# Both layernorms' normalised rows written with backward column chunks, and a new order of the units

## The chip, the core and the metric

The kernel runs on one core of one Trainium2 chip. The metric is the device time in microseconds (us), the median of several executions. Before the change it is 290.33 us (three runs, 290.32 to 290.42). One profiled execution took 287.78 us; inside it the hardware profiler's span, from the first recorded instruction to the last, is 286.0 us. Times of single instructions below come from that profile.

## The reference

One transformer block over 2048 tokens of 640 columns, in bf16. Cut to what matters:

```python
x = A_x                                          # [1, 2048, 640]
h = x + A(layernorm(x), wqkv, w_phi, wo)         # linear attention, 32 heads of 20
h2 = h + B(layernorm(h), w_gate, w_up, w_down)   # gated MLP, 1536 wide, no nonlinearity

# A: q, k, v = split(x @ wqkv); phi(q) = [softmax(q w_phi), softmax(-q w_phi)], phi(k) alike
#    kv = sum_s phi_k^T v;  z = sum_s phi_k;  o = (phi_q kv) / (phi_q z + 1e-6);  return o @ wo
# B: return ((x @ w_gate) * (x @ w_up)) @ w_down
```

The layernorm has no weights: (x - mean) / sqrt(var + 1e-5).

## The kernel before

The 2048 tokens are 16 tiles of 128 rows (NT); the 640 columns are 5 chunks of 128 (NC). Everything stays in on-chip memory between input and output.

The work of one tile t in the first part, with the names that the kernel gives to its units:

- L1s, L1a (VectorE, L398 to L401): mean and variance; L1l, L1e (ScalarE, L406, L409): 1/sqrt as exp(-0.5 ln v).
- xn (VectorE, L426): (x - mean) * rs, written as one row of 640 bf16 into one of four buffers.
- xt: transposes the row's five 128 x 128 blocks into xnT, chunk by chunk, so that the columns lie on the partitions. Tiles 0 to 2 on TensorE (L434, moved out of PSUM by xte), tiles 3 to 15 by a DMA transpose on SyncE's queue (L442).
- V and K (TensorE, L455): xnT's chunk c as the stationary operand, weight chunk c as the moving one, accumulated over c. For tiles 0 and 1 they are split into five units each (V0_0 to V0_4 and so on), so that each can start when its weight chunk is ready. K's and Q's weights are first multiplied by w_phi on the chip: WT transposes K's weights (L361), WTe moves them out of PSUM, F1 and F0 are the products (L382), Fe moves the result out.
- Ve moves V to SBUF; Kx makes both exponentials (ScalarE, L476); Ks and Kr are sum and reciprocal (VectorE, L479, L482); Kn divides (GpSimd, L484); KV adds the tile's phi_k^T v into three PSUM banks that live through all 16 tiles (TensorE, L493).

The second part: Q (L514) with its exponentials Qx; per tile N, the two numerator products (L547), a chain of small VectorE units (sr, rho, A, B, dd, rd), the division o (L579), a DMA transpose oT (L584), O times wo (L590), the residual h (L594), statistics L2s, L2a, and hc (ScalarE, L609): mean - h, written into the same four row buffers as xn. hT (L614) transposes it by DMA into xnT. The MLP runs over blocks of 256, 512, 512, 512 and 256 tokens: U (L629) gives gate and up products, g copies one (L634), u multiplies both (L637), D is the down product (L648), y scales by the row's -1/std and adds the residual (L660), w stores (L662).

The order is planned when the program is built. Each unit is entered with an engine, a cost (occupancy and latency in us), what it reads and writes, and a key. A table of text, TUNED, gives the key of each of 975 units, and with ":1" that the second of its possible engines is used. schedule (L687) is a list scheduler: it walks through modelled time, and whenever an engine is free it takes the ready unit with the lowest key. The keys are planned start times, so the engines' queues follow them. emit then puts semaphore waits between the queues; each engine works through its queue strictly in order, so a unit that waits holds up all behind it. The modelled costs never reach the chip; only the order and the choice of engine do. The function that gives the cost of a plain copy is the pattern for the others:

```python
def dve_c(n, psum=False):
    return 0.065 + n / 960.0 + (0.02 if psum else 0.0)
```

The functions that the change touches follow.

Of the kernel before, what the change touches and what calls it, by code (L numbers as in the profile page):

```python
# [12 lines left out]
P = 128  # L13
# [35 lines left out]
x0:0.7 wk0:4.06 wk2:3.58 wk4:2.14 x1:2.62 wv0:4.54 wv2:5.5 wv4:1.18 x2:5.02 x4:5.98 x6:6.46 phr:1.66 ph50:1 ph5:3.1 x8:15.6 x10:20.94 x12:26.78  # L49
x14:25.08 wqt0:25.56 wqt1:22.64 wqt2:31.25 wqt3:34.65 wqt4:38.91 wqt5:37.69 wo0:42.61 wo2:43.09 wg0:33.69 wu0:34.17 wg1:50.56 wu1:48.38 wg2:47.9  # L50
wu2:50.08 wg3:51.52 wu3:51.04 wg4:53.22 wu4:53.7 id0:0.7 gl0:1.2 eps:1.45 id1:2.97 gla0:3.97 glb0:4.41 gla4:1.87 glb4:2.31 gla1:1.65 glb1:4.19
gla2:2.09 glb2:2.75 gla3:2.53 glb3:4.63 phi0:4.85 phi5:6.053 va1:3.37 glx:6.304 kv1:6.704 zero:0.7 warm:1.08 WT0:7.553 WTe0:8.195 WT1:7.218
WTe1:8.902:1 WT2:6.883 WTe2:7.488 WT3:6.246 WTe3:6.851 WT4:4.63 WTe4:5.235 F1_0:9.36 Fe1_0:10.21:1 F1_1:9.933 Fe1_1:10.81 F1_2:10.507 Fe1_2:11.41:1
F1_3:7.916 Fe1_3:8.908:1 F1_4:6.581 Fe1_4:8.156 L1s0:3.163 L1a0:4.193 L1s1:5.583 L1a1:6.613 L1s2:10.51 L1a2:12.36 L1s3:9.66 L1a3:12.21 L1s4:14.2
L1a4:16.05 L1s5:11.36 L1a5:15.05 L1s6:12.51 L1a6:16.2 L1s7:15.2 L1a7:16.35 L1s8:19.58 L1a8:20.98 L1s9:21.13 L1a9:23.38 L1s10:24.93 L1a10:27.73
L1s11:25.78 L1a11:27.88 L1s12:32.77 L1a12:36.44 L1s13:38.54 L1a13:41.21 L1s14:41.36 L1a14:42.76 L1s15:35.02 L1a15:36.29 L1l0:4.523 L1e0:4.883
L1l1:6.943 L1e1:7.303 L1l2:12.69 L1e2:13.05 L1l4:16.68 L1e4:17.04 L1l8:28.21 L1e8:28.96 L1l12:43.091 L1e12:44.502 xn0:5.163 xt0:5.763 xte0:6.312
xn1:7.736 xt1:8.336 xte1:9.609 xn2:13.36 xt2:14.069 xte2:14.667 xn3:13.78 xt3:14.38 xn4:18.74 xt4:19.72 xn5:17.9 xt5:18.5 xn6:18.32 xt6:23.86 xn7:19.16
xt7:21.42 xn8:29.43 xt8:30.03 xn9:35.87 xt9:36.47 xn10:40.79 xt10:41.39 xn11:31.8 xt11:32.47 xn12:44.86 xt12:45.46 xn13:45.28 xt13:46.68 xn14:47.65
xt14:48.86 xn15:49.47 xt15:52 V0_0:9.088 V0_1:9.662 V0_2:10.235 V0_3:10.809 V0_4:11.352 Ve0:12.011 K0_0:11.08 K0_1:11.895 K0_2:12.439 K0_3:12.982  # L60
K0_4:13.525 Kx0_0:14.067 Kx0_1:15.268 Ks0:16.5 Kr0:20.43 Kn0:21.16 KV0:30.691 V1_0:12.71 V1_1:13.254 V1_2:13.797 V1_3:14.348 V1_4:14.891 Ve1:15.868
K1_0:11.624 K1_1:12.167 K1_2:14.619 K1_3:15.163 K1_4:20.911 Kx1_0:21.834 Kx1_1:22.644 Ks1:23.53 Kr1:27.18 Kn1:29.719 KV1:32.725 V2:16.836 Ve2:18.52
K2:15.478 Kx2_0:17.11 Kx2_1:17.92 Ks2:21.98 Kr2:26.63 Kn2:27.36 KV2:34.76 V3:19.553 Ve3:21.233 K3:18.194 Kx3_0:19.823 Kx3_1:20.633 Ks3:30.4 Kr3:32.22
Kn3:34.437 KV3:38.152 V4:26.616 Ve4:28.36 K4:23.899 Kx4_0:25.58 Kx4_1:26.39 Ks4:33.62 Kr4:37.99 Kn4:38.72 KV4:41.545 V5:21.183 Ve5:23.244 K5:22.541
Kx5_0:24.169 Kx5_1:24.98 Ks5:28.03 Kr5:29.85 Kn5:32.078 KV5:43.579 V6:27.974 Ve6:29.603 K6:31.367 Kx6_0:33.671 Kx6_1:34.482 Ks6:36.59 Kr6:42.21
Kn6:42.94 KV6:46.972 V7:25.258 Ve7:26.991 K7:29.333 Kx7_0:31.637 Kx7_1:32.447 Ks7:39.39 Kr7:44.31 Kn7:45.299 KV7:47.95 V8:33.401 Ve8:35.082 K8:35.436
Kx8_0:37.064 Kx8_1:37.874 Ks8:42.91 Kr8:47.1 Kn8:47.83 KV8:51.747 V9:42.221 Ve9:43.902 K9:40.187 Kx9_0:42.491 Kx9_1:43.301 Ks9:45.7 Kr9:50.44
Kn9:52.979 KV9:56.498 V10:45.614 Ve10:47.294 K10:44.255 Kx10_0:45.884 Kx10_1:46.694 Ks10:48.07 Kr10:49.89 Kn10:50.62 KV10:57.476 V11:36.794 Ve11:38.475
K11:38.828 Kx11_0:40.457 Kx11_1:41.267 Ks11:50.99 Kr11:52.57 Kn11:55.338 KV11:58.453 V12:52.423 Ve12:54.051 K12:49.03 Kx12_0:50.658 Kx12_1:51.469
Ks12:53.129 Kr12:54.709 Kn12:57.697 KV12:61.846 V13:55.139 Ve13:56.82 K13:50.388 Kx13_0:52.069 Kx13_1:52.879 Ks13:55.488 Kr13:57.068 Kn13:60.056  # L70
KV13:62.824 V14:60.488 Ve14:62.168 K14:53.781 Kx14_0:55.409 Kx14_1:56.22 Ks14:57.847 Kr14:59.427 Kn14:62.415 KV14:67.017 V15:63.5 Ve15:65.128:1
K15:59.129 Kx15_0:60.758 Kx15_1:61.568 Ks15:62.378 Kr15:63.958 Kn15:64.774 KV15:68.772 KVe0:69.718 KVe1:70.328 KVe2:70.938 F0_0:58.152 Fe0_0:58.723
F0_1:57.174 Fe0_1:57.746 F0_2:62.522 Fe0_2:63.094 F0_3:48.626 Fe0_3:49.198 F0_4:47.648 Fe0_4:48.22 Q0_0:70.527 Qx0_0_0:72.37 Qx0_0_1:71.876 Q0_1:65.937
Qx0_1_0:67.287 Qx0_1_1:67.78 Q0_2:69.448 Qx0_2_0:71.291 Qx0_2_1:70.797 Q0_3:67.693 Qx0_3_0:69.535 Qx0_3_1:69.042 Q0_4:64.858 Qx0_4_0:66.207
Qx0_4_1:66.701 Q1_0:78.727 Qx1_0_0:80.076 Qx1_0_1:80.57 Q1_1:87.595 Qx1_1_0:89.51 Qx1_1_1:89.016 Q1_2:82.309 Qx1_2_0:84.152 Qx1_2_1:83.659 Q1_3:86.516
Qx1_3_0:90.004 Qx1_3_1:88.523 Q1_4:75.879 Qx1_4_0:77.721 Qx1_4_1:77.228 Q2_0:77.648 Qx2_0_0:79.491 Qx2_0_1:78.997 Q2_1:92.881 Qx2_1_0:94.23
Qx2_1_1:94.724 Q2_2:73.03 Qx2_2_0:74.379 Qx2_2_1:74.873 Q2_3:91.112 Qx2_3_0:93.638 Qx2_3_1:92.461 Q2_4:90.033 Qx2_4_0:91.876 Qx2_4_1:91.382 Q3_0:79.806
Qx3_0_0:81.155 Qx3_0_1:81.649 Q3_1:84.747 Qx3_1_0:86.59 Qx3_1_1:86.096 Q3_2:74.799 Qx3_2_0:76.642 Qx3_2_1:76.149 Q3_3:71.606 Qx3_3_0:73.449
Qx3_3_1:72.955 Q3_4:80.885 Qx3_4_0:82.234 Qx3_4_1:82.728 wd0:96.508 wd1:95.068 wd2:96.028 wd3:95.548 N0_1:72.685 N0_0:74.109 sr0:73.3 rho0:74.724
A0:75.023 B0:75.988 dd0:76.953 rd0:77.251 o0:77.731 oT0:79.152 O0:83.389 h0:85.118 L2s0:86.049 L2a0:87.509 L2v0:88.96 L2r0:89.708 hc0:87.839 hT0:88.733  # L80
N1_1:77.303 N1_0:76.958 sr1:77.918 rho1:78.408 A1:78.706 B1:79.671 dd1:80.636 rd1:80.934 o1:81.414:1 oT1:82.326 O1:88.674 h1:90.486 L2s1:91.418
L2a1:92.448 L2v1:92.778 L2r1:93.128 hc1:92.955 hT1:93.848 N2_1:86.171 N2_0:85.826 sr2:86.899 rho2:87.659 A2:87.958 B2:88.923 dd2:89.888 rd2:90.186
o2:90.666 oT2:92.087 O2:95.664 h2:97.544 L2s2:98.476 L2a2:99.506 L2v2:99.836 L2r2:100.186 hc2:99.836 hT2:100.777 N3_1:81.964 N3_0:74.454 sr3:82.579
rho3:83.069 A3:83.368 B3:84.333 dd3:85.869 rd3:87.209 o3:87.689 oT3:89.953 O3:93.96 h3:95.643 L2s3:96.694 L2a3:98.296 L2v3:98.626 L2r3:99.326
hc3:98.664 hT3:99.557 N4_1:92.191 N4_0:92.536 sr4:92.806 rho4:93.296 A4:93.594 B4:94.559 dd4:95.524 rd4:96.394 o4:96.874 oT4:98.295 O4:106.256
h4:107.884 L2s4:109.368 L2a4:110.569 L2v4:110.899 L2r4:111.853 hc4:111.03 hT4:111.923 N5_1:99.205 N5_0:95.319 sr5:99.82 rho5:100.31 A5:100.609
B5:101.809 dd5:102.946 rd5:103.478 o5:103.958 oT5:105.379 O5:109.252 h5:111.101 L2s5:112.324 L2a5:113.525 L2v5:113.855 L2r5:114.455 hc5:114.034
hT5:114.927 N6_1:103.716 N6_0:103.371 sr6:104.331 rho6:104.821 A6:105.291 B6:106.256 dd6:107.221 rd6:107.519 o6:108.636:1 oT6:109.548 O6:114.575
h6:116.799 L2s6:117.73 L2a6:118.88 L2v6:120.331 L2r6:120.681 hc6:119.21 hT6:120.104 N7_1:133.568 N7_0:115.934 sr7:134.183 rho7:134.673 A7:134.971
B7:135.936 dd7:136.901 rd7:137.199 o7:137.679:1 oT7:138.591 O7:143.236 h7:144.908 L2s7:145.969 L2a7:146.999 L2v7:147.329 L2r7:147.934 hc7:147.329  # L90
hT7:148.223 N8_1:138.229 N8_0:140.733 sr8:139.118 rho8:141.643 A8:141.941 B8:142.906 dd8:144.309 rd8:144.608 o8:145.088 oT8:146.509 O8:151.782
h8:153.41 L2s8:154.342 L2a8:155.372 L2v8:155.702 L2r8:156.052 hc8:155.702 hT8:156.595 N9_1:144.939 N9_0:144.594 sr9:145.659 rho9:146.819 A9:147.149
B9:148.623 dd9:150.026 rd9:150.824 o9:151.304 oT9:152.725 O9:156.4 h9:158.029 L2s9:159.09 L2a9:160.12 L2v9:160.45 L2r9:161.055 hc9:160.45 hT9:161.344
N10_1:112.248 N10_0:112.593 sr10:113.675 rho10:114.337 A10:114.877 B10:116.014 dd10:117.55 rd10:118.58 o10:119.06 oT10:121.324 O10:161.709 h10:163.37
L2s10:164.854 L2a10:165.884 L2v10:166.214 L2r10:166.564 hc10:166.214 hT10:167.107 N11_1:176.039 N11_0:178.543 sr11:176.654 rho11:179.158 A11:179.456
# [106 lines left out]
def act_c(n, ptr=False):  # L202
    return (0.15 if ptr else 0.067) + n / 1200.0


def pool_c(n):
    return 0.183 + 0.0017 * n
# [801 lines left out]
```

## Time and profile before

| | |
|---|---|
| median time | 290.33 us |
| span of the profile | 286.0 us |
| TensorE busy, matmuls | 277.0 us, 2083 |
| VectorE busy | 184.4 us |
| ScalarE busy | 108.8 us |
| GpSimd busy | 58.9 us |
| xn (L426), 16 instructions | 13.0 us busy, mean 842 ns |
| hc (L609), 16 instructions | 13.1 us busy, mean 824 ns |
| Kn (L484), 16 instructions | 37.5 us busy, mean 2368 ns |

How to read the profile: it has a page (busy times, the span in slices, the chain of work that ended last, groups of instructions by line) and answers to questions about the trace. A line of the waits reads "engine, tile, line <- who ended the wait: us in total, times, longest". A line of the timeline reads "start, length, engine, line, operation, output <- input, shapes, count", with the idle time before it in brackets. PE is TensorE, PEld its weight loads, DVE VectorE, ACT ScalarE, POOL GpSimd, SPq SyncE's queue of transfers. Recorded matmuls overlap, so a busy TensorE may still be short of its best rate.

### The profile page before, as it was taken

The page shows a single profiled execution, that of the slowest core. Times are in us where ns is not written, and L with a number is a line of the kernel's source. Part 1 is how long each engine was busy: PE and PEld are TensorE (multiplying, and loading weights), DVE is VectorE, ACT ScalarE, POOL GpSimd, SP SyncE. Part 2 cuts the span into 40 slices and gives each one's busy share as a digit, 9 for nine tenths or more (in the row PEclk, how much of TensorE's full clock was granted, in tenths as well). Part 3 has the DMA queues.
Part 4 walks back from the last instruction along what each step waited for, and adds up shares of the span by engine and source line. Part 5 has one row for each costly group of instructions (what it writes and reads, how often), then busy time and mean ns, then how long its engine had stood idle before and what let it go on. Part 6 is the DMA issues. An engine that isn't in the chain of part 4 may idle for free.

```text
span 286.0 us, 5034 instructions
## 1 busy us (share of the span) xinstructions
PE 277.0 (97%) x2083; PEld 182.0 (64%) x2083; DVE 184.4 (64%) x364; ACT 108.8 (38%) x191; POOL 58.9 (21%) x66
## 2 busy tenths in 40 slices
PE   6899998999999999999999999998999999999996
PEld 2677776877555588854456774564456544678875
DVE  5799999985378888942588781587342373652342
ACT  4778555754877842321321112212340022022310
POOL 7003847699110321020003000001000000100000
PEclk9999999999999999999999999999999999999999
DMA  6737587990021397330013323015200110122002
GB/s 172 246 88 152 131 206 135 245 303 37 0 20 28 71 293 98 59 78 6 0 23 49 92 58 60 0 23 72 46 1 28 44 23 2 46 37 80 2 0 69
DMA packets 44832, 22.31 MB, mean 78 GB/s; under 512 B 35977, under 2 KB 43529, under 8 KB 44809
## 3 DMA queue, kind: packets, MB, share of 16 engines
q1 hardware_dynamic: 44809, 21.99, 33.5%
q8 instruction: 16, 0.26, 0.4%
q14 instruction: 7, 0.06, 0.1%
HBM read 11.00 MB, written 2.62 MB: 48 GB/s over the span
## 4 chain that ended last, share of the span: by engine, by line
PE 82%; DVE 6%; POOL 5%; DMA 4%; ACT 1%; issue 0%; SPq 0%; DVEq 0%; POOLq 0%
PE ps L629 36%; PE ps L648 18%; PE ps L514 8%; PE ps L455 7%; PE ps L590 7%; POOL ev L484 4%; PE ps L547 4%; DVE xn L426 3%; DVE SR L479 2%; DMA scratch<-scratch 2%; DMA scratch<-in_A_wqkv_dram 2%; DMA xnT<-xn 1%; PE ps L493 1%; DVE SR L482 1%; PE ps L382 1%; PE ps L361 1%
## 5 line engine op out<-in xcount | busy, mean ns | idle before, releaser
L629 PE MATMUL ps<-xnT,Wgu 128*128 128x512 bf16 (+1 forms) x600 | 107.8, 336 | 0.0
L629 PEld LDWEIGHTS ps<-xnT,Wgu 128*128 128x128 bf16 x600 | 58.3, 98 | 41.9 <-DVE ev L637 0.4
L634 ACT ACTIVATE scratch<-ps 128x512 bf16<-128x512 f32 (+1 forms) x60 | 30.7, 512 | 94.5 <-PE ps L629 84.7
L637 DVE TENSOR_TENSOR ev<-ps,scratch 128x512 bf16<-128x512 f32 (+1 forms) x60 | 33.4, 576 | 34.2 <-ACT scratch L634 23.5
L648 PE MATMUL ps<-Wp,ev 128*128 128x320 bf16 (+2 forms) x396 | 54.0, 295 | 0.0
L455 PE MATMUL ps<-Wp,xnT 128*128 128x320 bf16 x320 | 46.2, 299 | 1.5 <-DMA xnT<-xn 1.5
L648 PEld LDWEIGHTS ps<-Wp,ev 128*128 128x128 bf16 x396 | 38.0, 98 | 14.6
L484 POOL TENSOR_TENSOR ev<-ev,SR 128x1280 bf16<-128x1280 bf16 x16 | 37.5, 2368 | 27.9 <-DVE mv L401 16.7
L455 PEld LDWEIGHTS ps<-Wp,xnT 128*128 128x128 bf16 x320 | 30.2, 98 | 13.7 <-DMA xnT<-xn 2.4
L579 POOL TENSOR_TENSOR scratch<-scratch,sm 128x640 bf16<-128x640 f32 x10 | 12.7, 1273 | 123.7 <-DVE sm L576 110.2
L660 DVE SCALAR_TENSOR_TENSOR Wp<-ps,rs,x_all 128x640 bf16<-128x640 f32 (+3 forms) x18 | 14.6, 810 | 26.2 <-PE ps L648 26.1
L609 ACT ACTIVATE xn<-x_all,mv 128x640 bf16<-128x640 bf16 x16 | 13.1, 824 | 37.8 <-DVE mv L603 37.5
L476 ACT ACTIVATE ev<-ps 128x640 bf16<-128x640 f32 x32 | 21.0, 701 | 13.3 <-PE ps L455 9.2
L590 PE MATMUL ps<-Wo,scratch 128*128 128x320 bf16 x160 | 24.0, 299 | 1.3 <-DMA scratch<-scratch 1.3
L479 DVE TENSOR_REDUCE SR<-ev 128x64 f32<-128x1280 bf16 x16 | 23.4, 1461 | 2.8 <-ACT ev L476 2.1
L523 ACT ACTIVATE eqT<-ps 128x512 bf16<-128x512 f32 x40 | 21.7, 594 | 8.5 <-PE ps L514 8.5
L514 PE MATMUL ps<-xnT,Wp 128*128 128x512 bf16 x100 | 23.4, 379 | 0.0
L590 PEld LDWEIGHTS ps<-Wo,scratch 128*128 128x128 bf16 x160 | 15.5, 98 | 8.3 <-DMA scratch<-scratch 1.7
L560 DVE RECIPROCAL sm<-ps 128x32 f32<-128x32 f32 x16 | 5.6, 352 | 16.0 <-PE ps L547 15.9
L594 DVE TENSOR_TENSOR x_all<-ps,x_all 128x640 bf16<-128x640 f32 x16 | 13.1, 821 | 4.2 <-PE ps L590 4.1
L514 PEld LDWEIGHTS ps<-xnT,Wp 128*128 128x128 bf16 x100 | 9.5, 97 | 9.4
L547 PEld LDWEIGHTS ps<-KVm,eqT 128*128 128x128 bf16 x192 | 12.8, 98 | 4.1
(55 smaller groups left out, 204.6 us busy)
## 6 DMA issues: line engine op xcount, KB each, us to landing
out_dram<-Wp SPq DMA_DIRECT2D x15, 160.0 KB, 1.8
x_all<-in_A_x_dram SPq DMA_DIRECT2D x7, 320.0 KB, 4.2
Wgu<-in_B_w_gate_dram SPq DMA_DIRECT2D x5, 384.0 KB, 5.7
Wgu<-in_B_w_up_dram SPq DMA_DIRECT2D x5, 384.0 KB, 4.1
Wp<-in_B_w_down_dram SPq DMA_DIRECT2D x4, 480.0 KB, 5.7
scratch<-in_A_wqkv_dram SPq DMA_DIRECT2D x2, 320.0 KB, 4.8
Wp<-in_A_wqkv_dram SPq DMA_DIRECT2D x2, 320.0 KB, 5.8
Wo<-in_A_wo_dram SPq DMA_DIRECT2D x1, 480.0 KB, 4.3
```

The lines of the kernel that those rows point to most:

```text
L455: ins = e.matmul(pb(b, hb)[:, 0:320], lhsT=T["xnT"][:, c, P * t:P * (t + 1)], rhs=T["Wp"][:, kind, c, 320 * hb:320 * (hb + 1)], start=(c = ...
L476: G.op("act", "Kx%d_%d" % (t, s), lambda e, s=s, b=b, ek=ek: e.activation(out=T["ek"][:, ek.slots[0], s, :].rearrange("p (b n) -> p b n", ...
L479: G.op("dve", "Ks%d" % t, lambda e, ek=ek, sr=sr: e.tensor_reduce(out=T["SR"][:, sr.slots[0], 0, :], in_=T["ek"][:, ek.slots[0], :, :].rea ...
L484: G.op("pool", "Kn%d" % t, lambda e, ek=ek, sr=sr: e.tensor_tensor(out=T["ek"][:, ek.slots[0], :, :].rearrange("p s (h f) -> p (s h) f", f ...
L514: ins = e.matmul(pb(b)[:, 0:n], lhsT=T["Wp"][:, 0, i, P * c:P * (c + 1)], rhs=T["xnT"][:, i, o0:o0 + n], start=(i == 0), stop=(i == NC - 1))
L523: G.op("act", "Qx%d_%d_%d" % (q, c, s), lambda e, s=s, c=c, o0=o0, n=n, b=b: e.activation(out=T["eqT"][:, s, c, o0:o0 + n], in_=pb(b)[:, 0 ...
L547: ins = e.matmul(pb(b, y)[:, 22 * h0:22 * (h0 + j1 - j0)], lhsT=T["eqT"][:, s, c, P * t:P * (t + 1)], rhs=T["KVm"][:, OFF[s, c] + j0:OFF[s ...
L590: ins = e.matmul(pb(b, hb)[:, 0:320], lhsT=T["oT"][:, oT.slots[0], c, :], rhs=T["Wo"][:, c, 320 * hb:320 * (hb + 1)], start=(c == 0), stop ...
L629: ins = e.matmul(pb(b)[:, 0:n], lhsT=T["Wgu"][:, gu, c, P * ft:P * (ft + 1)], rhs=T["xnT"][:, c, o0:o0 + n], start=(c == 0), stop=(c == NC ...
L634: G.op("act", "g%d_%d" % (bi, ft), lambda e, pg=pg, gt=gt, n=n: e.activation(out=T["gt"][:, gt.slots[0], 0:n], in_=pb(pg)[:, 0:n], func=AF ...
L637: o_ = G.op("dve", "u%d_%d" % (bi, ft), lambda e, pu=pu, gt=gt, hh=hh, ft=ft, n=n: e.tensor_tensor(out=T["hh"][:, hh.slots[0], ft, 0:n], i ...
L648: ins = e.matmul(pb(b, hb)[:, 0:w], lhsT=T["hh"][:, hh.slots[0], ft, P * tt:P * (tt + 1)], rhs=T["Wd"][:, ft, c0 + w * hb:c0 + w * (hb + 1 ...
```

## The change

It has three parts.

First, the row that xn or hc writes has its five chunks in backward order: column chunk c goes to place 4 - c. The destination is therefore a pattern of five runs of 128 whose starts step downwards, where before it was one run of 640. The transposes are as before, so xnT now holds chunk c at place 4 - c, and every matmul that reads xnT takes chunk NC - 1 - c. It is meant to change how VectorE writes the row while GpSimd is at work.

```diff
+    def rev(b):
+        return T["xn"][:, b.slots[0], :].rearrange("p (c n) -> p c n", c=NC)[:, ::-1, :]
...
-            return e.tensor_scalar(out=T["xn"][:, xb.slots[0], :], in0=T["x"][:, t, :],
+            return e.tensor_scalar(out=rev(xb), in0=T["x"][:, t, :].rearrange("p (c n) -> p c n", c=NC),
                                    scalar1=T["mv"][:, t, 0:1], scalar2=T["rs"][:, t:t + 1], op0=ALU.subtract, op1=ALU.mult)
...
-                        ins = e.matmul(pb(b, hb)[:, 0:320], lhsT=T["xnT"][:, c, P * t:P * (t + 1)],
+                        ins = e.matmul(pb(b, hb)[:, 0:320], lhsT=T["xnT"][:, NC - 1 - c, P * t:P * (t + 1)],
...
-            out=T["xn"][:, hc.slots[0], :], in_=T["x"][:, t, :], func=AF.Identity, scale=-1.0, bias=T["mv2"][:, t, 0:1]),
+            out=rev(hc), in_=T["x"][:, t, :].rearrange("p (c n) -> p c n", c=NC), func=AF.Identity, scale=-1.0, bias=T["mv2"][:, t, 0:1]),
```

Q's and U's matmuls get the same index.

Second, the planner's costs are set anew, so that its modelled time is nearer to the chip's. Most are small; these are the kinds:

```diff
 def act_c(n, ptr=False):
-    return (0.15 if ptr else 0.067) + n / 1200.0
+    return (0.18 if ptr else 0.09) + n / 1200.0
...
-        pool_c(600), LP, [phr_b, gl_b[0]], [phi_b], -95)
+        0.72, LP, [phr_b, gl_b[0]], [phi_b], -95)
...
-             0.55, LD, [sr], [sr], kk)
+             0.46, LD, [sr], [sr], kk)
...
-                bw += o.dma / (240.0 if bw < 5.0 else 370.0)
+                bw += o.dma / (210.0 if bw < 7.0 else 370.0)
```

The VectorE copies of bf16 data out of PSUM are entered at half their size, A and B at 0.85 instead of 0.785 us, L1s and L2s at 0.82 instead of 0.85; xn stays at 0.42.

Third, all 975 keys are new, from a search over the planner with these costs. The beginning of TensorE's order, read from the keys:

```
before: warm WT4 xt0 WT3 F1_4 WT2 WT1 WT0 F1_3 xt1 V0_0 F1_0 V0_1 F1_1 V0_2 F1_2 V0_3 K0_0 V0_4 ...
after:  warm WT0 WT1 WT4 xt1 xt0 F1_0 F1_1 F1_4 WT2 WT3 K0_0 K1_0 K0_1 K1_1 F1_2 F1_3 V0_0 K0_2 ...
```

and of the loads on SyncE's queue (wk, wv are chunks of K's and V's weights, x tiles of the input):

```
before: x0 wv4 phr wk4 x1 ph5 wk2 wk0 wv0 x2 wv2 x4 x6
after:  x1 x0 phr wk0 ph5 wk4 wk2 x2 x6 wv0 wv4 wv2 x4
```

Other places that the text below speaks of, with the keys (planned starts in us):

| units | before | after |
|---|---|---|
| xn8, xn9, xn10, xn11 | 29.4, 35.9, 40.8, 31.8 | 30.9, 36.7, 31.3, 30.5 |
| xt8, xt9, xt10, xt11 (their transposes) | 30.0, 36.5, 41.4, 32.5 | 34.5, 37.4, 33.3, 31.1 |
| first use of each: V8 or K8, K9 or V9, K10 or V10, V11 | 33.4, 40.2, 44.3, 36.8 | 39.3, 42.0, 37.3, 34.5 |
| Kn2, Kn3, Kn5, Kn4 | 27.4, 34.4, 32.1, 38.7 | 27.4, 34.8, 37.1, 39.5 |
| Kn15; KV12, KV13, KV14 | 64.8; 61.8, 62.8, 67.0 | 63.3; 61.9, 62.9, 63.9 |
| last store before oT13, oT13, O13 | w5 188.4, 189.1, 192.0 | w3 190.3, 192.0, 196.3 |
| hT5, first U1 | 114.9, 119.5 | 122.4, 125.2 |
| hT7, first U2 | 148.2, 166.3 | 154.4, 157.9 |

## The prediction

> **What bounds the kernel now.** I read the page's shares first, then the chain that ended last, then the waits of TensorE alone, then the normalising line and the timelines around TensorE's gaps.
>
> ```profile
> span 286.0 us, 5034 instructions
> PE 277.0 (97%) x2083; PEld 182.0 (64%) x2083; DVE 184.4 (64%) x364; ACT 108.8 (38%) x191; POOL 58.9 (21%) x66
> PE 82%; DVE 6%; POOL 5%; DMA 4%; ACT 1%; issue 0%; SPq 0%; DVEq 0%; POOLq 0%
> ```
>
> TensorE is busy 97% of the span and the change takes no matmul away, so only its idle time can be won. How much is there? In the chain a matmul of 512 columns takes 0.216 us (10 of L629 in 2.16), one of 320 columns 0.136 (24 of L648 in 3.26), one of 256 columns 0.109; six of L547 take 0.36, twelve of L493 0.68, seven of L382 0.29, six transposes of L361 0.33. With the counts of the grouped lines: L629 360 x 0.216 + 240 x 0.109 = 103.9; L648 50.6 + 1.7 for the cut last tile; L455 320 x 0.136 = 43.5; L590 21.8; L514 21.6; L547 11.4; L493 10.9; folds and transposes 5.4; sum 270.8. The dense stream begins at 8.17 us and ends at 283.64: 275.5 us, so 4.7 us of holes, plus 8.2 us of start, plus a tail of 2.4 us. TensorE's waits name most of the holes:
>
> ```profile
> PE ps L361 <- DMA scratch<-in_A_wqkv_dram: 1.8, 2, 1.5
> PE ps L455 <- DMA xnT<-xn: 1.5, 2, 0.9
> PE ps L590 <- DMA scratch<-scratch: 1.3, 1, 1.3
> PE ps L493 <- POOL ev L484: 0.5, 2, 0.3
> ```
>
> The first is the start (weights of K arriving). The second is the first layernorm's rows arriving late through the DMA transpose. The third is one hole at 197.5 us in the MLP. The fourth is GpSimd's K normalisation. Why are the rows late?
>
> ```profile
> L426 DVE TENSOR_SCALAR xn<-x_all,mv,rs x16: 341/444/2482, 4.8 to 54.5; 128x640 bf16<-128x640 bf16 x16
> ```
>
> The same instruction takes 0.34 to 2.48 us. The two timelines show with what the long ones coincide (first VectorE, then GpSimd, 30 to 37 us):
>
> ```profile
> 30.76 2.48 DVE L426 TENSOR_SCALAR xn<-x_all,mv,rs 128x640 bf16<-128x640 bf16 x1 [0.56 <-ACT rs L409]
> 34.97 1.35 DVE L426 TENSOR_SCALAR xn<-x_all,mv,rs 128x640 bf16<-128x640 bf16 x1
> ```
>
> ```profile
> 28.39 4.67 POOL L484 TENSOR_TENSOR ev<-ev,SR 128x1280 bf16<-128x1280 bf16 x2 [4.07 <-DVE SR L482]
> 33.78 2.36 POOL L484 TENSOR_TENSOR ev<-ev,SR 128x1280 bf16<-128x1280 bf16 x1 [0.73 <-DVE SR L482]
> ```
>
> xn8 starts at 30.76 and ends at 33.24, just after GpSimd's pair ends at 33.06; xn11 starts at 34.97 and ends at 36.3, just after GpSimd's next ends at 36.14. The transpose of xn8 is issued at 33.27 and lands 2.6 us later; V8 starts at 35.92, after a hole of 0.58. xn9, queued on VectorE behind these, is written only at 39.63; its transpose lands at 43.72 and K9 starts at 43.76, after 0.88.
>
> ```profile
> 35.92 1.53 PE L455 MATMUL ps<-Wp,xnT 128*128 128x320 bf16 x10 [0.58 <-DMA xnT<-xn]
> 43.76 1.53 PE L455 MATMUL ps<-Wp,xnT 128*128 128x320 bf16 x10 [0.88 <-DMA xnT<-xn]
> ```
>
> [...] No row of before shows a backward write.
>
> **The change, part by part.**
>
> *Backward chunks.* xn's destination becomes 5 chunks of 128, stepping down, which can't be merged; the source is contiguous and can be read as one run of 640. [...] Removed: over the usual 0.44 us the long ones cost 0.77 (at 4.83, behind Phi's product), 2.04, 0.91, 0.13, 2.04 and 0.64: 6.5 us of VectorE. [...] Net 3.8 us of VectorE freed in the first 55 us, where the stage rows show it 94% busy (17.84 of 19.03 us, then 12.52 of 12.73). [...] The backward write of hc on ScalarE (0.82 us, 16 times) I cost at nothing: ScalarE is 38% busy. Matmuls reading chunk 4-c instead of c cost nothing: same shapes. The transposes move the same bytes.
>
> *Cost constants.* They emit no instruction; they and the keys only decide the order. I read the new order from the new keys, which are the planned starts; of their planned times I use only the distances between an issue and its use.
>
> *The order, start.* Before, wv4 and wk4 are requested early and wk2 lands at 8.12; until then TensorE has only WT4 and xt0 (0.6 us). After, x1, x0, phr, then wk0: 663 KB up to wk0 against 503 KB up to wk4, which landed at 5.05; 160 KB more at the 220 GB/s of these microseconds is 0.7 us, so WT0 at about 5.8. WT0, WT1, WT4, both xt and three folds (2.3 us) then lie before wk2's arrival. wk2 has 1145 KB up to it instead of 985: 160 KB at 300 GB/s, 0.5 us later, 8.6. From there to the end of V0, V1, K0, K1 and xt2: 20 x 0.272 + WT2, WT3 0.56 + F1_2, F1_3 0.58 + xt2 0.28 = 6.9 us; with before's 0.75 of bubbles in this stage, 16.2. Before, xt2 ends at 16.31 with five of the 20 products still to come: 16.31 + 5 x 0.272 = 17.7. **1.5 us** won, bounds 0 and 2.
>
> *The order, V and K.* xn8, xn10, xn11 come together at the point where GpSimd is between Kn2 and Kn3, and each transpose is issued 3.4 to 4.8 us ahead of its first use in the new keys, against 2.9 to 4.3 before; it needs 2.6 when the queue is free and 3.6 behind weight loads (40.08 to 43.72). The holes: 1.5 on L455, 0.24 more at 48.07 on its weight load, 0.5 on L493, and about 0.4 between folds and KV at 62.5 and 67.25. Of these 2.6 I count **2.0** as won: KV12 to KV14 still follow their Kn closely. New waits: K's chain on GpSimd is 16 x 2.36 = 37.8 us, and the new keys run it without pause from Kn3; behind a late Kn stand KV and everything after it on TensorE's in-order queue.
>
> *The order, MLP.* The 1.26 hole: oT13 is queued on SyncE behind w5, which waits for y5, which waits for D5. It is issued at 194.05, 0.38 behind the store w5, and lands 4.67 us later instead of 2.6. In the new keys oT13 stands 1.7 us behind a store and 4.3 us ahead of O13 (before 0.7 and 2.9). **1.26** won. But the new order has thin places of its own: U1's first product stands 2.8 us behind the issue of hT5 (a transpose takes 2.6 to 2.7), U2's 3.5 behind hT7. Each such slip costs up to 1 us. I charge **0.8** in all.
>
> *End.* D14 and the cut D15 swap; the last pieces, 192 and 128 columns, are the same: tail 2.4 us as before.
>
> Sum: 1.5 + 2.0 + 1.26 - 0.8 = 3.96 us off. 290.33 - 3.96 = 286.4.
>
> **Rivals.** (B) The engine still reads source and destination as 5 against 5[...] and waits for GpSimd[...]. Then the V and K holes stay and only start and MLP are won, less the new thin places: 1.5 + 1.26 - 0.8 = 2.0, 288.4. [...] (C) The new order opens holes of its own: Kn's unbroken run slips behind VectorE, KV waits 0.3 to 0.5 each for some six tiles (2.5 us), two transposes land late in the MLP (2 x 1.3, the size seen at 197.5); the start gains nothing as wv0 now comes after x2 and x6. 5.1 of new holes against 2.0 + 1.26 of old ones filled: 1.8 slower, 292.1. For it: the thin places counted above; before's own order shows such holes. (D) Start gains and new holes cancel, xn gains hide behind GpSimd: no change, 290.3.
>
> **How the numbers follow.** Forecast 0.65, B 0.15, C 0.14, D 0.06. Faster by over 0.2% (below 289.75) is the forecast and nearly all of B: 0.79. Same 0.06, slower 0.15. The low end takes all holes and a start of 2 us with no new ones: 2 + 2.6 + 1.26 = 5.9, of which I allow 5.3: 285.0. The high end includes B and D and leaves out most of C: 290.6.
>
> **What would show it.** xn's durations uniform, 0.5 to 0.6 us, max under 1, whatever GpSimd does, busy 8 to 10 us instead of 13.0; if its maximum is still over 2 us, B. No wait of L455 on xnT<-xn over 0.3; no wait of L590 on its transpose. First transposes of wk near 5.8 and V0 to K1 finished near 16.2. TensorE's busy time unchanged (277), its holes under 2 us after 16 us. Wrong would be: waits of L493 on L484 above 1 us, of L629 on a transpose, or a start later than before's.

## The result and the profile after

The changed kernel takes 285.73 us (median of four runs, 285.04 to 286.61) against 290.32 for the kernel before on the same chip: ratio 0.9855, 95% interval 0.9813 to 0.9897. Predicted were 286.4 us, range 285.0 to 290.6. Two later sets of runs on other chips gave 286.63 and 285.51 us, ratios 0.9868 (0.9823 to 0.9914) and 0.984 (0.9791 to 0.9888). The ratios leave out the slow executions, those over 1.5% above the fastest of their kernel, and so differ a little from the quotients of the medians. The forecast holds, and the experiments below ask whether its steps do. They do only in part: the largest step was too small, one was right by its number and wrong by its cause, and one was charged in the wrong place.

Line numbers after are six higher: xn is L432, V and K L461, Kn L490, KV L499, O L596, U L635, D L654, the transposes of K's weights L367.

The page of the changed kernel, its span, the busy times and the chain that ended last:

```profile
span 283.8 us, 5022 instructions
PE 274.8 (97%) x2066; PEld 182.1 (64%) x2083; DVE 182.5 (64%) x370; ACT 106.1 (37%) x187; POOL 56.8 (20%) x64
PE 78%; DVE 13%; DMA 5%; issue 1%; SPq 1%; POOL 1%; POOLq 0%; DVEq 0%
```

TensorE still sets the end. GpSimd, 5% of the chain before, is down to 1%; VectorE rose from 6% to 13%. The normalising line (minimum, median and maximum in ns, then first and last start):

```profile
L432 DVE TENSOR_SCALAR xn<-x_all,mv,rs x16: 508/597/606, 5.5 to 46.6; 128x640 bf16<-128x640 bf16 x16
```

No row takes over 0.61 us; before, the longest took 2.48. TensorE's waits, complete but for the warm-up's own:

```profile
PE ps L461 <- DMA xnT<-xn: 1.5, 2, 1.2
...
PE ps L367 <- DMA scratch<-in_A_wqkv_dram: 0.9, 1, 0.9
PE ps L461 <- ACT ev L482: 0.9, 1, 0.9
PE ps L461 <- DMA Wp<-in_A_wqkv_dram: 0.7, 1, 0.7
```

The wait in the MLP (1.3 us before) and those of KV on Kn (0.5) are gone, and the start waits 0.9 and not 1.8 us for K's weights. The waits of V and K on the transposed rows are not gone: 1.5 us as before, the longest now at V10, and there are two new ones, on ScalarE's exponentials and on V's weights. TensorE's timeline shows where they lie:

```profile
5.78 1.18 PE L367 MATMUL ps<-ident,scratch 128*128 128x128 bf16 x18 [0.94 <-DMA scratch<-in_A_wqkv_dram]
...
11.80 4.52 PE L461 MATMUL ps<-Wp,xnT 128*128 128x320 bf16 x32 [0.72 <-DMA Wp<-in_A_wqkv_dram]
...
32.34 1.53 PE L461 MATMUL ps<-Wp,xnT 128*128 128x320 bf16 x10 [0.93 <-ACT ev L482]
...
40.55 1.53 PE L461 MATMUL ps<-Wp,xnT 128*128 128x320 bf16 x10 [1.24 <-DMA xnT<-xn]
```

If the end of the products before them is counted at 0.136 us each, the two holes in V and K are 1.1 us (31.25 to 32.34, ahead of V6) and 1.4 us (39.16 to 40.55, ahead of V10): 2.5 us. What opens the first, and a part of the second, is seen on VectorE's timeline:

```profile
30.37 0.49 DVE L404 BATCH_NORM_STATS2 st<-x_all 128x6 f32<-128x320 bf16 x1 [0.83 <-DMA x_all<-in_A_x_dram]
...
32.63 1.63 DVE L432 TENSOR_SCALAR xn<-x_all,mv,rs 128x640 bf16<-128x640 bf16 x3
```

In the new order the statistics of tile 13 (L1s13) stand ahead of xn8, xn10 and xn11 on VectorE, and they wait for x12, the load of tiles 12 and 13 (issued at 26.46, landed at 30.34, 3.9 us later). The three rows were planned for 30.5 to 31.3 and start at 32.63. What hangs on them comes later: the transposes of tiles 8, 10 and 11, and, through L1a11 behind the same wait and the logarithm on ScalarE, the exponentials of K5 that V6 waits for.

The hole ahead of V10 has a second part. In the new order the transpose of tile 10 stands on SyncE's queue right behind two loads of MLP weights, 384 KB each. It is issued at 35.62 and lands at 40.51, 4.9 us later, where the prediction had allowed for 2.6 to 3.6. No run below moves these loads, so how the hole is shared between the late row and the slow transpose stays open.

### The profile page after: what moved, and what is told of

It is laid out like the page before. It is cut to its first block, busy times and chain, and to the rows that moved or that the text cites. A ratio compares the mean times of both kernels' runs of the same rounds, so it can differ in the third digit from the quotient of the medians.

```text
span 283.8 us, 5022 instructions
## 1 busy us (share of the span) xinstructions
PE 274.8 (97%) x2066; PEld 182.1 (64%) x2083; DVE 182.5 (64%) x370; ACT 106.1 (37%) x187; POOL 56.8 (20%) x64
## 4 chain that ended last, share of the span: by engine, by line
PE 78%; DVE 13%; DMA 5%; issue 1%; SPq 1%; POOL 1%; POOLq 0%; DVEq 0%
PE ps L635 36%; PE ps L654 18%; PE ps L596 8%; PE ps L520 6%; DVE SR L485 4%; PE ps L553 4%; DMA x_all<-in_A_x_dram 3%; PE ps L461 3%; DVE xn L432 2%; PE ps L499 2%; DVE st L405 2%; DVE st L404 2%; DMA xnT<-xn 1%; DVE SR L488 1%; SPq L268 1%
## 5 line engine op out<-in xcount | busy, mean ns | idle before, releaser
L635 PE MATMUL ps<-xnT,Wgu 128*128 128x512 bf16 (+1 forms) x587 | 106.5, 335 | 0.7
L635 PEld LDWEIGHTS ps<-xnT,Wgu 128*128 128x128 bf16 x600 | 58.2, 98 | 42.2 <-DVE ev L643 0.4
L654 PE MATMUL ps<-Wp,ev 128*128 128x320 bf16 (+2 forms) x396 | 54.1, 295 | 0.0
L461 PE MATMUL ps<-Wp,xnT 128*128 128x320 bf16 x320 | 46.0, 299 | 3.2 <-DMA xnT<-xn 1.5
L654 PEld LDWEIGHTS ps<-Wp,ev 128*128 128x128 bf16 x396 | 38.0, 98 | 14.3
L490 POOL TENSOR_TENSOR ev<-ev,SR 128x1280 bf16<-128x1280 bf16 x16 | 37.3, 2359 | 24.9 <-DVE SR L488 19.3
L461 PEld LDWEIGHTS ps<-Wp,xnT 128*128 128x128 bf16 x320 | 30.5, 98 | 15.4 <-DMA xnT<-xn 2.3
L610 POOL TENSOR_SCALAR ln<-mv 128x1 f32<-128x1 f32 x16 | 3.9, 245 | 115.7 <-DVE mv L609 112.1
L596 PE MATMUL ps<-Wo,scratch 128*128 128x320 bf16 x160 | 24.0, 299 | 0.0
L520 PE MATMUL ps<-xnT,Wp 128*128 128x512 bf16 x96 | 22.3, 379 | 0.2
L596 PEld LDWEIGHTS ps<-Wo,scratch 128*128 128x128 bf16 x160 | 15.6, 98 | 7.5
L585 POOL TENSOR_TENSOR scratch<-scratch,sm 128x640 bf16<-128x640 f32 x8 | 10.2, 1272 | 44.8 <-DVE sm L582 42.2
L553 PE MATMUL ps<-KVm,eqT 128*128 128x154 bf16 (+1 forms) x192 | 15.5, 221 | 0.1
```

The costliest lines, as they stand in the source:

```text
L461: ins = e.matmul(pb(b, hb)[:, 0:320], lhsT=T["xnT"][:, NC - 1 - c, P * t:P * (t + 1)], rhs=T["Wp"][:, kind, c, 320 * hb:320 * (hb + 1)], s ...
L490: G.op("pool", "Kn%d" % t, lambda e, ek=ek, sr=sr: e.tensor_tensor(out=T["ek"][:, ek.slots[0], :, :].rearrange("p s (h f) -> p (s h) f", f ...
L520: ins = e.matmul(pb(b)[:, 0:n], lhsT=T["Wp"][:, 0, i, P * c:P * (c + 1)], rhs=T["xnT"][:, NC - 1 - i, o0:o0 + n], start=(i == 0), stop=(i ...
L553: ins = e.matmul(pb(b, y)[:, 22 * h0:22 * (h0 + j1 - j0)], lhsT=T["eqT"][:, s, c, P * t:P * (t + 1)], rhs=T["KVm"][:, OFF[s, c] + j0:OFF[s ...
L596: ins = e.matmul(pb(b, hb)[:, 0:320], lhsT=T["oT"][:, oT.slots[0], c, :], rhs=T["Wo"][:, c, 320 * hb:320 * (hb + 1)], start=(c == 0), stop ...
L635: ins = e.matmul(pb(b)[:, 0:n], lhsT=T["Wgu"][:, gu, c, P * ft:P * (ft + 1)], rhs=T["xnT"][:, NC - 1 - c, o0:o0 + n], start=(c == 0), stop ...
```

## The experiments

The ratios are to the kernel before on the same chip. "Backward alone" and "order alone" are the two halves of the change.

**The kernel before, looked at again.** No edit.

> The kernel before, unchanged, profiled once more: its executions lie between 287.8 and 290.4 us and the first profile caught the fastest. Theory [...]: what differs between executions is which of xn and Kn starts first, so the long xn are other ones or longer ones (sum of the L426 row not 13.0 us) and the holes of TensorE before 70 us differ by 1 to 2 us. Rival (transfers at the start): the first dense matmul moves from 8.17 us by 1 to 2 us and the xn row stays at 13.0 us.

Measured: 288.28 us. Rows up to 2.48 us again, and a wait of 1.9 us in the MLP. Of 33 other executions of this kernel in this set (286.97 to 291.69, median 289.47) only four were faster, so it doesn't show what a slow one looks like. The rows took 12.6 us in all (13.0 in the first trace) and the dense stream began at 8.07 (8.17), so neither the theory nor the rival is shown.

**Backward rows alone, in the old order.**

```diff
-            return e.tensor_scalar(out=T["xn"][:, xb.slots[0], :], in0=T["x"][:, t, :],
+            return e.tensor_scalar(out=rev(xb), in0=T["x"][:, t, :].rearrange("p (c n) -> p c n", c=NC),
...
-                        ins = e.matmul(pb(b, hb)[:, 0:320], lhsT=T["xnT"][:, c, P * t:P * (t + 1)],
+                        ins = e.matmul(pb(b, hb)[:, 0:320], lhsT=T["xnT"][:, NC - 1 - c, P * t:P * (t + 1)],
```

(with the same for hc, Q and U; keys and costs as before)

> The kernel before with the backward rows alone, its order and costs untouched. Theory: all 16 xn take 0.5 to 0.61 us as in the changed kernel, none waits for GpSimd, VectorE is freed of some 4 us; V8's hole of 0.58 us goes and K9's of 0.88 shrinks, the hole at 197.5 us stays: 288 to 289 us. Rival (the new order does it all): xn is uniform but the transposes come as late as before and the time stays within 0.3 us of 290.3.

Measured: 285.99 us, ratio 0.9891 (0.9848 to 0.9934). The rows, and TensorE's waits:

```profile
L430 DVE TENSOR_SCALAR xn<-x_all,mv,rs x16: 508/596/606, 4.8 to 52.2; 128x640 bf16<-128x640 bf16 x16
```

```profile
PE ps L365 <- DMA scratch<-in_A_wqkv_dram: 2.1, 2, 1.8
...
PE ps L594 <- DMA scratch<-scratch: 1.2, 1, 1.2
PE ps L459 <- DMA xnT<-xn: 0.7, 3, 0.3
```

In the old order the waits on the rows are down to 0.7 us in all, none over 0.3, and those of KV are gone: what the prediction expected of the whole change holds for this half of it. The start and the MLP's hole stay. This half alone brings 3.5 us at the median (3.2 by the ratio), more than the 1.3 to 2.3 that its theory expected.

**The new order alone, with forward rows.** The changed kernel with the old writes of xn and hc and the old chunk index:

```diff
-            return e.tensor_scalar(out=rev(xb), in0=T["x"][:, t, :].rearrange("p (c n) -> p c n", c=NC),
+            return e.tensor_scalar(out=T["xn"][:, xb.slots[0], :], in0=T["x"][:, t, :],
```

> The changed kernel with forward rows: new order and costs alone. Theory: xn is again 0.34 to 2.5 us, and as the new order runs Kn without pause from 37 to 56 us, the six xn that fall into it or beside it wait up to 2.4 us each; 1 to 3 us slower than the changed kernel, 287 to 289 us. Rival [...]: 285.7 us within 0.5, with long xn that nobody waits for.

Measured: 288.16 us, ratio 0.9934 (0.9904 to 0.9965): 1.3 us at the median (1.9 by the ratio). Its rows again take up to 2.48 us. The MLP's wait is gone, and a wait of 1.8 us on the exponentials is there. The 17 times fall into two groups, 285.3 to 286.7 (six) and 287.8 to 289.0 (eleven). The trace is of the fastest, so what parts the two groups stays open.

**Five runs on both sides.** The kernel before, with xn's source read and its destination written backward: five runs of 128 each. Same bytes, same engine, same order; only the counts of source and destination are now equal at five. Each row is written backward from a source read backward, so its columns stay in forward order. The question is whether the step downwards by itself frees the row from GpSimd or whether the source in one run is needed.

```diff
-            return e.tensor_scalar(out=T["xn"][:, xb.slots[0], :], in0=T["x"][:, t, :],
+            return e.tensor_scalar(out=rev(xb), in0=T["x"][:, t, :].rearrange("p (c n) -> p c n", c=NC)[:, ::-1, :],
```

> The kernel before with xn's source and destination both read and written with backward chunks, 5 runs against 5, so that the row itself stays forward; hc and all else as before. Theory [...]: xn is as long as before, maximum over 2 us, and the time is 290.3 within 0.7. Rival [...]: xn is uniform at 0.5 to 0.61 us and the time is that of the backward rows alone.

Measured: 289.92 us, ratio 1.0011 (0.9979 to 1.0043). The rows, and one of them on VectorE's timeline:

```profile
L430 DVE TENSOR_SCALAR xn<-x_all,mv,rs x16: 373/469/2511, 4.8 to 57.1; 128x640 bf16<-128x640 bf16 x16
```

```profile
33.02 2.51 DVE L430 TENSOR_SCALAR xn<-x_all,mv,rs 128x640 bf16<-128x640 bf16 x1 [0.56 <-ACT rs L413]
```

and GpSimd in these microseconds:

```profile
30.65 4.67 POOL L488 TENSOR_TENSOR ev<-ev,SR 128x1280 bf16<-128x1280 bf16 x2 [3.98 <-DVE SR L486]
```

A backward write by itself changes nothing: the row takes 2.51 us and ends at 35.53, just after GpSimd's pair at 35.32. With the same write and a source that can be read as one run of 640, no row takes over 0.61 us. Why the first form is held up and the second is not was not shown: the traces print only the shapes (128x640), not how source and destination are encoded, and two differences are not separated from each other. Here there are five runs on both sides, in the changed kernel a source that can be one run against five; and there source and destination run in opposite directions, here in the same. No run has unequal counts in one direction.

This trace, of an execution with a span of 290.7 us, the slowest of its 15, also has TensorE wait 4.4 us for transposed rows, where the kernel before's own trace has 1.5.

**The load x12 earlier.** The changed kernel with two keys moved, so that x12 stands ahead of a weight transpose on SyncE's queue and tile 13's statistics behind those of tile 11 on VectorE (only the two keys of the changed lines are shown):

```diff
-x12:25.347
+x12:23.7
...
-L1s13:28.157
+L1s13:31.765
```

> The changed kernel with two keys moved: the load x12 is requested ahead of the weight transpose wqt0 instead of behind it, and the statistics L1s13, which wait for it, stand behind Ks4 and L1a11 instead of ahead of them. Theory (the new order's two holes at 31.3 us, 1.1 us, and 39.2 us, 1.4 us, are both VectorE's queue standing before x12): both go or shrink below 0.4, 1.5 to 2.4 us faster than the changed kernel run beside it. Rival (the holes come from VectorE being full, not from the load): they move behind other tiles and the time stays within 0.5 us.

**The changed kernel again**, beside it on the same chip. No edit.

> The changed kernel once more, beside the others on one chip. 285.0 to 286.6 us as before; holes at 31.3 and 39.2 us again, no hole after 70 us, first weight transposes at 5.8 us at full clock.

Measured: 285.84 (ratio 0.985, 0.9801 to 0.9898) with the early load, 286.63 without. V6's wait is gone, which is what the theory of that run says; the waits on transposed rows stay (1.3 us in three, none over 0.6), which is what its rival says. The gain is 0.8 us with overlapping intervals. Its trace can't settle where xn8's group would start, since this execution was about 1.5 us late by the end of its first 18 transposes: they began at 6.42 and took 2.10 us (5.78 and 1.18 in the changed kernel's first trace). A later run takes this up.

**A filler in the old order.** The kernel before with five matmuls of 512 zero columns behind the first transpose of xn0, where TensorE waits for wk2:

```diff
+    def fill(e):
+        for _ in range(5):
+            ins = e.matmul(pb(fl_b)[:, 0:512], lhsT=T["zero"][:, 0:P], rhs=T["zero"][:, :], start=True, stop=True)
+        return ins
+    G.op("pe", "fill", fill, 0.05, LT, [z_b], [fl_b], 6.0)
```

> The kernel before with five matmuls of zeros, 512 columns each, put behind xt0 on TensorE, where it waits for wk2 until 8.1 us; nothing reads them. Theory (in part of its executions the kernel before loses its full clock in that wait and runs the weight transposes at half speed, 2.09 instead of 1.17 us for 18): the clock stays full, the slower executions go and the median falls by 0.7 to 1.5 us. Rival (the executions differ by their transfers): the median stays within 0.4 us of the kernel before and the spread of about 4 us with it.

**Backward alone, again**, on the chip of these three, to tell how much of the change is the rows and how much the order.

> The backward rows alone in the old order once more, beside the changed kernel on one chip. Theory [...]: 286 us, within 0.7 us of the changed kernel. Rival [...]: at least 1.2 us slower than the changed kernel.

Measured: the filler 288.28 us, ratio 0.9934 (0.9911 to 0.9957); backward alone 286.57, ratio 0.9877 (0.9833 to 0.992), level with the changed kernel's 286.63. Five useless matmuls bring 2.5 us at the median, more than the 0.7 to 1.5 of their theory, and by the ratio (1.9 us) as much as the order alone. Why? One part is the clock. In the old order TensorE idles from 5.9 to 7.8 us, and in part of the executions the granted clock is half for a stretch after this pause. The stage rows of backward alone (the first set) show it in the column ahead of the last two, the granted clock:

```profile
6.00:8.00 2.00, 0.26 (x5) 0.26 (x6) 0.60 (x2) 1.44 (x4) 0.63 (x2) 1.00 0.98 322
8.00:10.00 2.00, 2.00 (x27) 2.00 (x24) 1.71 (x3) 0.61 (x1) 0.00 (x0) 0.55 0.93 286
10.00:12.00 2.00, 2.00 (x24) 1.91 (x23) 0.90 (x3) 1.53 (x3) 0.00 (x0) 0.59 1.02 366
```

and TensorE's timeline of the same trace has the transposes of the next weight chunks in these microseconds:

```profile
8.54 2.09 PE L365 MATMUL ps<-ident,scratch 128*128 128x128 bf16 x18
```

The 18 transposes take 2.09 us; in the filler's trace they take 1.17. The two rows with 0.55 and 0.59 come to 3.4 us at half rate ((0.45 + 0.41) x 2 us / 0.5), and this execution's mean clock is 0.994, as 3.4 us at half rate in 287 would make it. Of the executions of the kernel before, 23 of 33 in the first set and 20 of 27 on the filler's chip have a mean clock of 0.988 to 0.994. Of the 22 with the filler 6 do, of the changed kernel's 12 in both later sets none.

But a mean of 1.0 does not prove a start at full rate: two traces with that mean (x12 early and the third one of the changed kernel) run these 18 transposes in 2.10 us, and the next 12 in the 0.83 us that the changed kernel's first trace has too.

What sets the clock back in one execution and not in another was not shown. With 3.4 us at half rate, at most 1.7 us of work can be lost; the 18 transposes show 0.9 of it.

But 0.9 is not 1.9 to 2.5. The other part stands in the waits of the filler's trace, complete but for the warm-up's own:

```profile
PE ps L462 <- DMA xnT<-xn: 4.3, 3, 2.7
...
PE ps L368 <- DMA scratch<-in_A_wqkv_dram: 0.6, 1, 0.6
```

The rows are as late as ever. The wait in the MLP, though, is gone, while oT13 still stands 0.38 us behind the store w5, as it did in the kernel before. The prediction had put that wait down to the store. The transfers in the 4 us around it tell more. In backward alone (chip of the filler's run; the store is issued at 191.98, oT13 at 192.36), in slices of 0.1 us, and then the queues and the landings:

```profile
GB/s 0 0 0 0 0 0 0 0 0 218 358 371 333 256 90 13 51 351 225 205 207 192 161 61 5 0 0 3 8 10 8 8 10 10 10 105 255 0 0 0
...
q8 instruction: 1, 0.02, 1.7%
...
out_dram<-Wp SPq DMA_DIRECT2D x1, 160.0 KB, 1.9
scratch<-scratch SPq DMA_TRANSPOSE x1, 4.7
```

First the store, then the transpose at 200 GB/s, and then, for 0.7 us, a trickle of 8 to 10 GB/s. One packet of queue q8 lies upon the transpose, a fetch of 16 KB of instructions (1.7% of 16 engines x 4 us, 1.1 us of one engine). It runs from 193.61 to 194.70, and the trickle begins as it ends; so it does, within 0.2 us, in the other four traces with this hole.

The page names q8 "instruction", with 16 packets and 0.26 MB, 16 KB each. TensorE has 2083 matmuls and 2083 weight loads, one packet for 260. That they are TensorE's instructions is inferred from this count, and tested below by adding ten.

In all five traces of the old order without added instructions (two of the kernel before, two of backward alone, one of five to five), a q8 packet starts 0.6 to 1.4 us after oT13's issue, oT13 takes 4.6 to 5.3 us, and TensorE waits 1.2 to 1.9. The clock does not part them: the mean clock is 1.0 and 0.999 in the kernel before's two traces, 0.994 in backward alone's two, 1.0 in five to five's. With the filler the packet lies 2.0 us ahead of oT13's issue, and oT13 takes 3.4.

**The changed kernel with the early load and ten warm-up matmuls.** **Backward alone with the filler.** **The changed kernel a third time.** All three on one chip; the first two are the edits above put together, with

```diff
-NWARM = 8
+NWARM = 10
```

in the first.

> The changed kernel with x12's load two places earlier (as in the run with x12 early) and ten warm-up matmuls instead of eight. A cold warm-up matmul took 0.45 us, so the warm-up ends near 5.7 us instead of 4.83, just ahead of the first weight transpose at 5.8. Theory (the late load of x12 costs the changed kernel about 1 us at V6, and TensorE's short pause before the first transposes now and then costs it the full clock): 0.8 to 1.2 us below the changed kernel on the same chip, all runs at mean clock 1.0. Rival (VectorE is full up to 47 us, so what is taken from V6's hole comes back at the transposes of xn8 and xn9; the clock holds anyway): within 0.3 us of the changed kernel.

> The old order with backward rows, plus five matmuls of 512 zero columns behind the first transpose of xn0, where TensorE otherwise waits for wk2. Theory (the filler's 2.5 us on the kernel before had two parts, the clock at the start and a start whose phase suits the rows of xn; with backward rows only the clock is left): 0.6 to 1.0 us below backward rows alone, which gave 286.0 and 286.6, so 285.3 to 285.9, with mean clock 1.0. Rival 1 (the clock alone was worth the 2.5 us): 284.1. Rival 2 (the clock does nothing to the time): 286.6 or above.

> The changed kernel again, beside the other two on the same chip. 286.2 (it gave 285.7 and 286.6), ratio to before 0.985 to 0.988. If backward rows with the filler stand level with it or below it, the new order brings nothing that five matmuls of filler don't; if it stands 0.5 us or more below them, the hole in the MLP that the old order keeps (1.2 to 1.9 us) is what the order is worth.

Measured: 285.36 (284.64 to 285.72), 284.01 (283.30 to 284.38) and 285.51 us (284.52 to 287.55); ratios 0.984 (0.9798 to 0.9883), 0.9794 (0.9752 to 0.9836), 0.984 (0.9791 to 0.9888). The early load with the longer warm-up is level with the changed kernel, as its rival said. The hole at V6 is closed, but 1.9 us of waits on xnT are left, the longest 1.3 (1.5, 1.6 and 1.8 in the changed kernel's three traces). xn8's group starts at 32.73; in the changed kernel it starts at 32.63, and at 33.66 and 34.14 in the two later traces, where x12 came later. Nothing on VectorE waits for x12 any more ahead of it: the statistics of three tiles and a sum stand there. The stage rows from 30 to 48 us show it, first of this kernel, then of backward alone with the filler (busy time of TensorE, its weight loads, VectorE, ScalarE, GpSimd):

```profile
30.00:48.00 18.00, 16.07 (x147) 11.81 (x145) 18.00 (x33) 9.97 (x19) 13.05 (x7) 1.00 0.82 151
```

```profile
30.00:48.00 18.00, 18.00 (x177) 14.08 (x175) 16.46 (x30) 10.51 (x19) 14.50 (x7) 1.00 0.97 186
```

In the new order VectorE has no idle time at all here and TensorE 1.9 us; in the old order TensorE has none and VectorE 1.5. In the changed kernel's three traces too VectorE's only idle time in these 18 us is its wait for x12 (0.4 to 1.4 us). So the new order leaves VectorE no slack here, and a row that is late stays late. It is not the whole of what is left: the wait of 1.3 us ends with a transpose that stands behind a weight load and takes 5.3 us to land (issued at 40.25; the products that wait for it start at 45.57).

The old order with backward rows and five useless matmuls beats the changed kernel by 1.5 us, without overlap of their times. Its waits:

```profile
PE ps L372 <- DMA scratch<-in_A_wqkv_dram: 1.8, 1, 1.8
...
PE ps L466 <- DMA xnT<-xn: 0.7, 1, 0.7
```

The expectation of it (285.3 to 285.9) failed; the number is that of its rival 1, the clock alone (284.1). But the filler again takes the MLP's wait away. And the pause at the start is still there, as the 1.8 us show: the filler lasts only 1.3 us here (2.3 in the filler's first trace), yet the mean clock is 0.999 to 1.0 in all six executions. Is the MLP's wait gone by the ten instructions, or by the clock and the phase of the start?

**Ten instructions without the filler.** Backward alone, with five small matmuls right behind the warm-up. They add the same five matmuls and five weight loads to TensorE's stream, but leave the pause:

```diff
+        for _ in range(5):
+            ins = e.matmul(pb(wm_b)[:, 0:128], lhsT=T["zero"][:, 0:P], rhs=T["zero"][:, 0:P], start=True, stop=True)
```

> The old order with backward rows, plus five zero matmuls of 128 columns right behind the eight of the warm-up. They add the same ten TensorE instructions (five matmuls, five weight loads) as the filler did, but do not fill the wait for wk2: 0.11 us each at the half clock, so the warm-up ends near 5.4 us and the pause up to 7.8 stays. Theory (the hole of 1.2 to 1.9 us before O13 is a 16 KB fetch of TensorE's instructions that falls upon oT13's transpose behind the store w5; ten more instructions ahead of it move the fetch ahead of the store): the fetch lies ahead of the store, oT13 lands in about 3.5 us instead of 4.7, no wait of TensorE on scratch<-scratch, half clock at the start still in some of the runs, 1.0 to 1.3 us below backward rows alone (286.0 and 286.6), so 285.1, ratio to before near 0.984. Rival (the filler took the hole away by the phase or the clock of the start): the wait of 1.2 to 1.3 us on scratch<-scratch is still there, 286.3, ratio 0.988.

Measured: 284.17 us (283.26 to 285.25), ratio 0.9852 (0.982 to 0.9885). The same view as above, the store issued at 191.34 and oT13 at 191.72:

```profile
GB/s 0 0 0 0 0 0 0 0 77 320 358 320 371 154 39 10 120 210 207 220 228 202 207 175 139 3 0 0 0 0 0 0 0 0 0 0 0 0 0 0
...
out_dram<-Wp SPq DMA_DIRECT2D x1, 160.0 KB, 1.8
scratch<-scratch SPq DMA_TRANSPOSE x1, 3.4
```

No q8 packet in these 4 us (it starts at 189.73, 2.0 us ahead of oT13's issue, where it was 0.6 and 1.3 behind in backward alone's two traces), no trickle, 3.4 instead of 4.7 us, and TensorE's waits name no transpose in the MLP. Order, store and distances are those of backward alone. So the hole goes with an instruction fetch upon a transpose that a store already delays; the store alone costs 0.8 us over 2.6, which the order leaves room for. The pause is still there (1.6 us), as expected. Three of the six executions have a mean clock of 0.994 (284.17 to 285.25), three of 1.0 (283.26 to 284.17), 1.5 us apart at the median. How much of the time is the clock's isn't settled by that: for the kernel before, executions below 1.0 are slower by 0.8 us at the median in the first set and faster by 1.4 in the third. How much the moved fetch alone brings isn't clear of the noise either: this run was on another chip than backward alone, and the medians differ by 2.4 us, the ratios (0.9877 and 0.9852) by 0.7; the wait taken away is 1.2 to 1.3.

## Why the prediction was right, and where it was not

**What bounds the kernel.** Right: the gains and losses that the traces name are holes of TensorE, or its clock.

**Backward chunks.** Right in effect and size. The rows take 0.51 to 0.61 us whatever GpSimd does, 9.1 us in all in backward alone (8 to 10 expected, 13.0 before): 0.15 over the usual 0.44, and 3.9 us of VectorE freed, where 3.8 were expected. The time added to a row was the author's estimate, which no trace of before shows; nor does any run show why the row is freed. Writing hc backward costs ScalarE nothing that shows (826 against 824 ns), and ten matmuls of V or K still take 1.53 us. Rival B is out: the rows are uniform, and the five-to-five run shows what B would look like (rows up to 2.51 us). One reading was loose: the stage rows that were to show the first 55 us cover 31.8 of them, 96% busy; the 55 us are 87% busy (47.83).

**V and K, 2.0 us.** The mechanism was right for the rows, the term too small. Backward alone brings 3.5 and 4.2 us at the medians (3.2 and 3.6 by the ratios). The 2.6 us of holes, from which the 2.0 came, were read from one execution of 287.78 us, when the median was 290.33. In the other forward-row traces of the old order, of 292.4 us (five to five, the slowest of 15) and 288.3 us (filler, at its median), the waits on xnT alone were 4.4 and 4.3; with backward rows they are 0.7 and 0.5. No typical execution of the kernel before itself was traced, so that it has such waits too is inferred. The sign was to be had beforehand: the profiled time stood 2.5 us under the median.

**The start, 1.5 us.** Half right. The first weight transposes begin at 5.78, as predicted (5.8). The end of V0 to K1 and xt2 comes at 16.9 and not 16.2: V's weights wv0, now behind x2 and x6, land late and cost 0.72 us (1.28 in the second run of the changed kernel), where all bubbles of this stage had been taken as 0.75. So 0.8 of the 1.5. What the step did not have is the clock. The new order waits 0.7 to 1.6 us here (0.2 with ten warm-up matmuls) where the old one waits 1.5 to 1.9, and the mean clock of its 45 executions, with and without edits, is 0.999 to 1.0; but in two of its six traces the first 18 transposes took 2.10 us all the same.

**The MLP, 1.26 us.** The number came out, the reason did not. The prediction said that oT13 lands late as it is queued 0.38 us behind the store. Three runs with that same distance have no hole; the store alone makes oT13 land in 3.4 to 3.5 us, and the fetch makes that 4.6 to 5.3. In the new order no fetch meets oT13 (a q8 packet at 191.5, oT13 at 196.06, landed in 2.6 us), which the prediction did not count on: that this term came out is luck in part. The new order also has O13 start 4.4 us after oT13's issue, where the old one could have at 3.5, so it might have borne a fetch; no run tests that.

**The thin places, 0.8 us.** Failed in place and size. TensorE has no wait over 0.15 us after 70 us; hT5 and hT7 land in time. The new holes are 2.5 us in V and K. They come from VectorE, which the new order leaves without slack from 30 to 48 us (busy for all 18 us but its wait for x12, against 16.46 in the old order with backward rows and filler), and from transposes behind weight loads. The prediction looked at the keys for the distance from transpose to use, and from Kn to KV. It did not add up what stands on VectorE ahead of the rows, and took 3.6 us for a transpose behind weight loads where tile 10's took 4.9. The expectations of "no wait of L455 over 0.3" and of holes under 2 us after 16 us fail for the changed kernel (1.2, and 2.4 in all); the first holds for backward rows in the old order in one of their two traces (0.3) and not in the other (0.5).

**The sum.** -3.96 predicted, -4.6 measured (-4.1 and -4.2 in the later sets): two errors, the rows' gain too small by 1.2 to 2.2 us and the new holes too small by about 1.7, lie against each other, so that the total came so close is luck. On top of backward rows the new order brings nothing that can be measured (286.57 against 286.63 on one chip): its gains at the start and in the MLP are paid back in V and K. The rival C, an order that opens holes of its own, was right as to their kind; it named KV and the MLP's transposes, not the statistics.

**Open:** what parts the two groups of times of the order alone; whether the clock at the start alone makes the spread of the kernel before (286.97 to 293.28 over both sets), since executions with a mean clock of 1.0 lie near both ends (286.97 and 291.80; a mean that can hide 18 transposes in 2.10 us); whether VectorE's load or the slow transposes hold V10 longer; and whether the counts or the directions of source and destination free the row.

## What to carry to other kernels

A VectorE row that runs beside GpSimd can be freed from it as here: a contiguous source, and a destination of five chunks in backward order. Five backward chunks on both sides did not do it (rows up to 2.51 us, against 0.61). It cost 0.15 us for 640 columns; do this first, alone, before a new order. Compare the profiled execution's time with the median before you add up its holes: one that is 2.5 us faster is likely to show fewer of them than the kernel mostly has. Where one transfer lands late for no reason in its queue, look for an instruction fetch among the packets around it: ten instructions ahead of it moved the fetch here, and a hole of 1.3 us was gone. The best version measured, backward rows and five filler matmuls in the old order, takes 284.01 us, 2.1% below the kernel before.

## What the runs showed of the hardware

A DMA transpose that meets a 16 KB instruction fetch (0.9 to 1.8 us for one packet) lands later: oT13, 0.38 us behind a store of 160 KB, lands in 3.4 to 3.5 us without it (three traces) and in 4.6 to 5.3 with it (five). Where no other transfer is near, a transpose of 128x640 after 78 us lands in 2.6 us, and in 2.8 to 3.6 if a fetch starts 0.2 to 0.7 us after its issue (five such cases: issued at 83.67, 114.55 and 170.12 in the trace of the kernel before, at 83.22 and 129.66 in that of the changed one).

With TensorE pausing for 1.5 to 1.9 us soon after a warm-up of eight matmuls, most executions of the kernel before (54 of 82) have a mean clock of 0.988 to 0.994; in backward alone's trace, with 0.994, it is 3.4 us at half rate after this pause. In the trace of the changed kernel's third run the first 18 transposes took 2.10 instead of 1.18 us, and the 21 matmuls of the folds behind them 1.58 instead of 1.06: this execution took 287.55, the others of the set 284.52 to 286.16.
